# Splitting x2 one token tile at a time, and moving z's load, sums and split to steps 3, 7 and 11 of 16

## The chip, the core and the metric

One NeuronCore of a Trainium2 chip runs the whole program. The metric is device time in microseconds (us), lower is better, given as the median over several runs. TensorE (PE) multiplies, VectorE (DVE), ScalarE (ACT) and GpSimd (POOL) work elementwise, and SyncE (SP) issues nearly all DMA transfers. Each engine takes its instructions strictly in the order in which they are written, and semaphores tie the engines together.

## What is computed

The reference, cut to what matters, with x of 8 x 3072 x 256 values and 24,576 tokens after the transform:

```python
X = np.fft.fft(np.fft.fft(x, axis=1), axis=2).real          # 8 x 3072 x 256
x1 = X.reshape(24576, 256)
h = x1 @ w_in                                                # 256 -> 2048
x2 = (h - np.tanh(h)) @ w_out                                # 2048 -> 256
h2 = x2 @ w_in2                                              # 256 -> 1024
e = np.exp(h2 - h2.max(-1, keepdims=True))
solu = h2 * e / (e.sum(-1, keepdims=True) + 1e-9)
ln = (solu - solu.mean(-1)) / np.sqrt(solu.var(-1) + 1e-6) * g_ln
out = ln @ w_out2                                            # 1024 -> 256
```

## The kernel before

**Stages.** The first stage (24 rounds `q`, some 195 us) computes the Fourier transform over the 3072 positions and leaves its result, z, in DRAM; it also folds the other transform into `w_in` and prepares the weights. The second stage takes the rest of the time: 48 groups `n` of 256 columns of z. One column makes two tokens, so a group is 512 tokens, or four token tiles `i` of 128. Six groups make one batch entry.

**Pieces of twice the precision.** Every matmul is done in three passes on float32r operands, as hi x hi, hi x lo and lo x hi. So every operand has to be split: ACT rounds it (`rnd`, line 151), and POOL or DVE subtracts the rounded part from the whole (`rest`, line 154). Nearly all subtractions in the second stage are POOL's; they all have line 155 in the profile and are told apart by the tile that they write: `gh` (the activations of the first layer pair), `ut` (those of the second), `x2s` (x2) and `zs` (z).

**Steps.** A group has 16 steps `j`, one for each 128 of the 2048 features, and the loop at line 969 writes 768 steps out by hand. In each step PE makes `ab` from the group's `zs` (line 736). DVE makes `h` from it (lines 747 to 763), ACT takes the tanh (line 769), DVE makes `g` (line 774), ACT and POOL split it into `gh`, and two steps later PE adds its product with `w_out` to the group's x2, held in PSUM as `x2p` (function `o1`, line 793). When the sixteenth is in, ACT copies `x2p` to SBUF as `x2f` (line 810), and x2 is split into `x2s`.

**The second layer pair runs one group behind, in cycles of four steps**, one cycle for each token tile. By the remainder q of the step number by 4, PE's order is:

- q = 0: `ab`, `o1`, then the first half of `h2` (line 826, stationary operand `x2s`)
- q = 1: `ab`, the second half of `h2`, `o1`
- q = 2 and 3: `ab`, one half of the last product `po` (line 916, stationary operand `ut`), `o1`

The other engines follow. In q = 0, ACT squares (line 856) and rounds the first `ut`; on POOL the five small instructions of `scale` (lines 863 to 869) need the result of that square, and the first `ut` subtraction stands behind them. `ut` comes from a transposition by way of DRAM (`turn`: one store to `mv_d`, then four loads to `um`). In q = 3, ACT scales the output `o` and SP stores it. A tile's first `h2` is in steps 4, 8, 12 of the next group and 0 of the one behind that.

**z** comes from DRAM to `zf` (function `load_z`, three transfers issued by SP). In three of six groups, those with index 0, 1 and 2 in the batch entry, even and odd parts first have to be added and subtracted on POOL (four instructions of 128 columns, tile `zc`), because the transform leaves them apart; in the other three `zf` is used as it is. Then both 256-column halves u are split into `zs`. All this is for group n + 1 and is done during group n: the load in step 6, the two halves in steps 9 and 11, each with its own sums ahead of it.

**x2** of group n is split at the end of step 1 of group n + 1: two roundings and two subtractions of 128 x 512.

Of the kernel before, what the change touches and what calls it, by code (L numbers as in the profile page):

```python
# [127 lines left out]
def fft2_moe_moe_kernel(  # L128
# [94 lines left out]
    def load_z(n):  # L223
# [13 lines left out]
        zs = zp.tile([P, 2, 2, GP], F32R, tag="zs", name=f"zs{n}")  # L237
        zg[n] = (zf, nb, zs)

    def split_z(n, u):  # L240
        zf, nb, zs = zg[n]
        if n % GPB >= NSJ:
            split_halves(nc.gpsimd, zs[:, 0, u], zs[:, 1, u], zf[:, u])
        else:
            zc = zp.tile([P, GP], F32, tag="zc", bufs=1, name=f"zc{n}_{u}")
            for w, op in enumerate((ALU.add, ALU.subtract)):
                nc.gpsimd.tensor_tensor(out=zc[:, w * P : (w + 1) * P], in0=zf[:, u, :P], in1=zf[:, u, P:], op=op)
            split_halves(nc.gpsimd, zs[:, 0, u], zs[:, 1, u], zc)


    coming, raws = [], {}
# [332 lines left out]
    for q in range(NQ):  # L584
        b, j = divmod(q, NSJ)
        ending = now[:]
        now.clear()
        works = []
        if ahead <= q + 2 < NQ:
            works.append(prep(q + 2))  # L590
        works += ready
        weave(*works)
        weave(*ending)
        ready = coming_weights(q + 1)
        if folds and j == 0:
            fold_w_in(*folds.pop())
        if q == 3:
            transform_nu()
        transform(q)
        if j == NSJ - 1 and q < NQ - 1:  # L600
            evict(b)
        if q == 13:
            for n in range(2):
                load_z(n)
        if q in (15, 16, 17, 18):
            split_z(*divmod((15, 16, 17, 18).index(q), 2))
        if q == NQ - 4:
            nc.sync.dma_start(out=wnu, in_=wnu_d.rearrange("o (m p) -> p (o m)", p=P))
            nc.sync.dma_start(
                out=nu_h, in_=nu_d[:, PAIRS : PAIRS + 1].rearrange("b o -> o b").to_broadcast([P, B])  # L610
            )
# [113 lines left out]
    nc.vector.memset(mhalf, -0.5)  # L725

    hs, ts_, gs = {}, {}, {}
    x2p, x2s = {}, {}

    def ab(n, m):  # L730
        _, nb, zs = zg[n]
# [53 lines left out]
    def o1(n, m):  # L785
        if m == 0:
            x2p[n] = [p_x2.tile([P, 2 * GP], F32, tag=f"x2_{mt}", name=f"x2p{n}_{mt}") for mt in range(2)]
        gh = gs.pop((n, m))
        c, k = divmod(m, 4)

        for i, (hw, hg) in enumerate(((0, 0), (1, 0), (0, 1))):
            for mt in range(2):
                nc.tensor.matmul(  # L793
                    in_pairs(x2p[n][mt]),
                    wo1[c][:, hw, k, mt * P : (mt + 1) * P],
                    in_turn(gh[:, hg]),
                    start=(m == 0 and i == 0),
                    stop=(m == NM - 1 and i == 2),
                )
        if m == NM - 1:  # L800
            xs = wk.tile([P, 2, 2, 2 * GP], F32R, tag="x2s", name=f"x2s{n}")
            x2s[n] = xs
            if n == NG - 1:
                for mt, p in enumerate(x2p.pop(n)):
                    rnd(xs[:, 0, mt], p)
                    rest(nc.vector, xs[:, 1, mt], p, xs[:, 0, mt])
                return
            xf = wk.tile([P, 2, 2 * GP], F32, tag="stage", name=f"x2f{n}")
            for mt, p in enumerate(x2p.pop(n)):
                rnd(xf[:, mt], p)  # L810
            for mt in range(2):
                rnd(xs[:, 0, mt], xf[:, mt])
                rest(nc.gpsimd, xs[:, 1, mt], xf[:, mt], xs[:, 0, mt])

    h2s, es, us, sts, uts, pos, moved = {}, {}, {}, {}, {}, {}, {}

    def h2(n, i, f):
        xs = x2s[n]
        if f == 0:
            h2s[n, i] = taken(bank_h2, [P, FF2], "h2", f"ph2_{n}_{i}")  # L820
        ph = h2s[n, i]
        tk = slice(i * P, (i + 1) * P)
        fs = slice(f * 512, (f + 1) * 512)
        for k in range(2):
            for q, (hx, hw) in enumerate(PASSES):
                nc.tensor.matmul(  # L826
                    in_pairs(ph[:, fs]),
                    xs[:, hx, k, tk],
                    in_turn(wi2[:, hw, k, fs]),
                    start=(k == 0 and q == 0),  # L830
                    stop=(k == 1 and q == 2),
                )
# [98 lines left out]
    def tile_at(step, back):  # L931
        t = (step - NM - back) // 4
        return divmod(t, 4) if 0 <= t < 4 * NG else None
# [35 lines left out]
    for step in range(steps + 2):  # L969
        n, j = divmod(step, NM)  # L970
        if step < steps:
            pab = ab(n, j)
            asb = lead(n, j, pab) if n == 0 else None

        lag = 2 if step < NM else 1
        for s in range(out_done, min(step - lag + 1, steps)):
            act_out(*divmod(s, NM))
        out_done = max(out_done, min(step - lag + 1, steps))
        if step < steps:
            act_in(n, j, pab, asb or lead(n, j, pab))  # L980
# [12 lines left out]
        if step in (10, 12):
            split_wi2((step - 10) // 2)
        if step in (2, 3):
            load_wo2(step - 2)
        if step == 6:
            split_special()
        if 8 <= step < NM:
            gain_wo2(step - 8)  # L1000
        if NM + 2 < step <= NM + 6:
            special_out(step - NM - 3, pa)
        if step == NM:
            cm = mean_wo2()
        if step == NM + 1:
            for half in range(2):
                center_wo2(half, cm)
        if NM + 2 <= step < NM + 6:
            pa = special(step - NM - 2)
        if NM + 2 <= step < NM + 4:  # L1010
            split_wo2(step - NM - 2)
        if j == 6 and 1 <= n and n + 1 < NG:
            load_z(n + 1)
        if 1 <= n and n + 1 < NG and j in (9, 11):
            split_z(n + 1, int(j > 9))


    first.close()
# [81 lines left out]
```

## Time and profile before

| | |
|---|---|
| median of 3 runs | 2838.28 us (2837.79 to 2838.76) |
| the profiled execution | 2839.47 us |
| its span, first to last instruction | 2837.7 us |
| mean granted TensorE clock over the span | 0.996 of full speed |
| PE busy (matmul) | 2742.0 us, 97% |
| DVE / POOL / ACT busy | 84% / 69% / 64% |

The span is what the trace covers; the execution is 1.8 us longer. Idle time of an engine that nobody waits for costs nothing, so the questions are where PE waits, for whom, and why that engine is late.

### The profile page before, as it was taken

The numbers are of one execution on the slowest core, as the hardware profiler recorded it, in microseconds if no ns is written. First come the engines' busy times: TensorE is split into PE (matmuls) and PEld (weight loads), VectorE is DVE, ScalarE is ACT, GpSimd is POOL, SyncE is SP. The second block draws the span as 40 slices with busy tenths as digits, with TensorE's granted clock in tenths as the row PEclk, the third lists the DMA queues.
The fourth block names the chain that finished last, engine by engine and source line by source line (L and its number), as shares of the span: only waits on it lengthen the run. The fifth ranks groups of instructions, "written<-read, shape, count | busy, mean of one in ns | idle before, by whom it ended". The sixth has DMA issues, their size and how long they took to land. (4 is left out here: it accounts for less than half of the span.)

```text
span 2837.7 us, 50135 instructions
## 1 busy us (share of the span) xinstructions
PE 2742.0 (97%) x16799; PEld 2442.4 (86%) x16799; DVE 2394.9 (84%) x4818; ACT 1806.2 (64%) x3287; POOL 1950.6 (69%) x2413
## 2 busy tenths in 40 slices
PE   7899999999999999999999999999999999999998
PEld 4467999889988899889988898889998899888998
DVE  7897888888888888888888888888888888888885
ACT  2336666666666666666666666666666666666665
POOL 0146777777777777777777777777777777777773
PEclk9999999999999999999999999999999999999999
DMA  8780444344434344344434443444434343344441
GB/s 315 241 326 22 97 93 98 91 96 99 96 90 103 90 97 97 90 97 96 99 90 97 97 96 92 101 91 97 97 90 97 90 103 92 95 98 95 94 92 46
DMA packets 876513, 303.77 MB, mean 107 GB/s; under 512 B 788520, under 2 KB 837688, under 8 KB 872960
## 3 DMA queue, kind: packets, MB, share of 16 engines
q1 hardware_dynamic: 873536, 293.95, 41.8%
q10 hardware_dynamic: 2304, 6.29, 0.6%
q8 instruction: 133, 2.18, 0.4%
q14 instruction: 124, 1.02, 0.1%
q0 software_dynamic: 416, 0.33, 0.0%
HBM read 162.01 MB, written 138.47 MB: 106 GB/s over the span
## 5 line engine op out<-in xcount | busy, mean ns | idle before, releaser
L155 POOL TENSOR_TENSOR gh<-g,gh 128x512 fp32r<-128x512 f32 x768 | 984.1, 1285 | 367.4 <-ACT gh L152 357.1
L793 PE MATMUL x2p<-gh,wo 128*128 128x512 f32 x4608 | 1141.6, 381 | 35.8 <-POOL gh L155 22.4
L793 PEld LDWEIGHTS x2p<-gh,wo 128*128 128x128 f32 x4608 | 821.3, 190 | 156.0 <-POOL gh L155 64.5
L769 ACT ACTIVATE t<-h 128x512 f32<-128x512 f32 x768 | 459.1, 598 | 467.6 <-DVE h L763 378.9
L774 DVE TENSOR_TENSOR g<-h,t 128x512 f32<-128x512 f32 x768 | 521.9, 680 | 189.1 <-ACT t L769 183.6
L736 PEld LDWEIGHTS ab<-zs,wt 128*128 128x128 f32 x4608 | 632.9, 191 | 44.2 <-PE ab L736 2.8
L736 PE MATMUL ab<-zs,wt 128*128 128x256 f32 x4608 | 638.8, 275 | 2.3 <-DVE h L763 2.3
L152 ACT ACTIVATE gh<-g 128x512 fp32r<-128x512 f32 x768 | 480.3, 625 | 230.8 <-DVE g L774 228.9
L916 PE MATMUL po<-wo,ut 128*128 128x256 f32 x4608 | 588.5, 276 | 28.1 <-POOL ut L155 24.4
L916 PEld LDWEIGHTS po<-wo,ut 128*128 128x128 f32 x4608 | 549.2, 192 | 37.1 <-POOL ut L155 31.6
L826 PE MATMUL ph<-wi,x2s 128*128 128x512 f32 x2304 | 559.8, 379 | 0.0
L155 POOL TENSOR_TENSOR ut<-um,ut 128x512 fp32r<-128x512 f32 x372 | 478.1, 1285 | 0.9 <-issue 0.9
L747 DVE SCALAR_TENSOR_TENSOR asb<-nb,wnu,ab 128x256 f32<-128x256 f32 x768 | 365.9, 476 | 127.4 <-PE ab L736 120.9
L826 PEld LDWEIGHTS ph<-wi,x2s 128*128 128x128 f32 x2304 | 421.2, 189 | 51.5
L763 DVE TENSOR_TENSOR h<-asb,ab 128x256 f32<-128x256 f32 x768 | 329.5, 429 | 26.5
L762 DVE TENSOR_TENSOR h<-asb,ab 128x256 f32<-128x256 f32 x768 | 329.2, 429 | 26.1
L839 ACT ACTIVATE e<-ph,st 128x1024 f32<-128x1024 f32 x192 | 214.3, 1116 | 88.2 <-PE x2p L793 49.3
L837 DVE TENSOR_REDUCE st<-ph 128x1 f32<-128x1024 f32 x192 | 233.6, 1217 | 3.2 <-PE ph L826 3.2
L845 DVE SCALAR_TENSOR_TENSOR u<-ph,e 128x1024 f32<-128x1024 f32 x192 | 233.5, 1216 | 0.0
L152 ACT ACTIVATE ut<-um 128x512 fp32r<-128x512 f32 x372 | 230.8, 621 | 0.0
L876 DVE STREAM_TRANSPOSE tb<-u 128x1024 f32<-128x1024 f32 x186 | 230.0, 1237 | 0.0
L856 ACT ACTIVATE e<-u,st 128x1024 f32<-128x1024 f32 x192 | 219.7, 1144 | 0.0
(101 smaller groups left out, 1544.0 us busy)
## 6 DMA issues: line engine op xcount, KB each, us to landing
mv_d<-tb SPq DMA_DIRECT2D x186, 512.0 KB, 2.6
um<-mv_d SPq DMA_DIRECT2D x744, 128.0 KB, 3.8
out<-o SPq DMA_DIRECT2D x192, 128.0 KB, 1.7
x<-xr SPq DMA_DIRECT2D x23, 1024.0 KB, 7.8
z_d<-zt ACTq DMA_DIRECT2D x16, 384.0 KB, 6.6
z_d<-zt SPq DMA_DIRECT2D x16, 384.0 KB, 7.5
wo<-w_out SPq DMA_DIRECT2D x24, 256.0 KB, 5.5
zf<-z_d SPq DMA_DIRECT2D x48, 128.0 KB, 3.4
```

What stands on the lines that cost most here:

```text
L152: nc.scalar.activation(out=o, in_=i, func=AF.Copy)
L155: eng.tensor_tensor(out=o, in0=i, in1=hi.bitcast(F32), op=ALU.subtract)
L736: nc.tensor.matmul(in_pairs(pab[:, u]), wt[c][:, hw, u, o : o + P], in_turn(zs[:, hz, u]), start=(i == 0), stop=(i == 2),)
L747: nc.vector.scalar_tensor_tensor(out=asb, in0=zg[n][1], scalar=wnu[:, m : m + 1], in1=pab[:, 0], op0=ALU.mult, op1=ALU.add)
L762: nc.vector.tensor_tensor(out=h[:, 0], in0=asb, in1=pab[:, 1], op=ALU.add)
L763: nc.vector.tensor_tensor(out=h[:, 1], in0=asb, in1=pab[:, 1], op=ALU.subtract)
L769: nc.scalar.activation(out=t, in_=h, func=AF.Tanh)
L774: nc.vector.tensor_tensor(out=g, in0=hs.pop((n, m)).rearrange("p u n -> p (u n)"), in1=ts_.pop((n, m)).rearrange("p u n -> p (u n)"), op=A ...
L793: nc.tensor.matmul(in_pairs(x2p[n][mt]), wo1[c][:, hw, k, mt * P : (mt + 1) * P], in_turn(gh[:, hg]), start=(m == 0 and i == 0), stop=(m = ...
L826: nc.tensor.matmul(in_pairs(ph[:, fs]), xs[:, hx, k, tk], in_turn(wi2[:, hw, k, fs]), start=(k == 0 and q == 0), stop=(k == 1 and q == 2),)
L837: nc.vector.tensor_reduce(out=st[:, 0:1], in_=ph, axis=AX.X, op=ALU.max, negate=True)
L916: nc.tensor.matmul(in_pairs(po[:, :D]), ut[:, hu, ks], in_turn(wo2[:, hw, k]), start=(k == 0 and q == 0), stop=(k == NK2 - 1 and q == 2),)
```

## The change

x2 is no longer split in one go. `x2f` is still copied out in step 1, but every step with q = 3 now ends with the split of the one token tile that `h2` takes in the following step: one rounding and one subtraction of 128 x 256 (two blocks of 128). `x2s` becomes a tile of 128 tokens in four buffers. For the last group, where no steps follow, the split is made straight from PSUM, still in one go but tile by tile (eight roundings and eight subtractions of 128 columns in place of two of 512).

For z, the load moves from step 6 to step 3, all four sums to step 7, and both halves' splits to step 11, behind that step's piece of x2. `zc` gets two buffers. In the first stage the sums of both halves now stand ahead of the first half's split.

```diff
+    zc = {}
+    def sum_z(n):
+        if n % GPB >= NSJ:
+            return
+        zf = zg[n][0]
+        for u in range(2):
+            zc[n, u] = zp.tile([P, GP], F32, tag="zc", name=f"zc{n}_{u}")
+            for w, op in enumerate((ALU.add, ALU.subtract)):
+                nc.gpsimd.tensor_tensor(
+                    out=zc[n, u][:, w * P : (w + 1) * P], in0=zf[:, u, :P], in1=zf[:, u, P:], op=op
+                )
     def split_z(n, u):
         zf, nb, zs = zg[n]
...
-            zc = zp.tile([P, GP], F32, tag="zc", bufs=1, name=f"zc{n}_{u}")
-            for w, op in enumerate((ALU.add, ALU.subtract)):
-                nc.gpsimd.tensor_tensor(out=zc[:, w * P : (w + 1) * P], in0=zf[:, u, :P], in1=zf[:, u, P:], op=op)
-            split_halves(nc.gpsimd, zs[:, 0, u], zs[:, 1, u], zc)
+        split_halves(nc.gpsimd, zs[:, 0, u], zs[:, 1, u], zc.pop((n, u), zf[:, u]))
...
         if q in (15, 16, 17, 18):
-            split_z(*divmod((15, 16, 17, 18).index(q), 2))
+            n, u = divmod((15, 16, 17, 18).index(q), 2)
+            if u == 0:
+                sum_z(n)
+            split_z(n, u)
...
         if m == NM - 1:
-            xs = wk.tile([P, 2, 2, 2 * GP], F32R, tag="x2s", name=f"x2s{n}")
-            x2s[n] = xs
...
-            xf = wk.tile([P, 2, 2 * GP], F32, tag="stage", name=f"x2f{n}")
+            xf = x2f[n] = wk.tile([P, 2, 2 * GP], F32, tag="stage", name=f"x2f{n}")
             for mt, p in enumerate(x2p.pop(n)):
                 rnd(xf[:, mt], p)
-            for mt in range(2):
-                rnd(xs[:, 0, mt], xf[:, mt])
-                rest(nc.gpsimd, xs[:, 1, mt], xf[:, mt], xs[:, 0, mt])
+    def x2s_tile(n, i):
+        x2s[n, i] = wk.tile([P, 2, 2, P], F32R, tag="x2s", bufs=4, name=f"x2s{n}_{i}")
+        return x2s[n, i]
+    def split_x2(n, i):
+        xs, xf = x2s_tile(n, i), x2f[n][:, :, i * P : (i + 1) * P]
+        rnd(xs[:, 0], xf)
+        rest(nc.gpsimd, xs[:, 1], xf, xs[:, 0])
...
-        if j == 6 and 1 <= n and n + 1 < NG:
-            load_z(n + 1)
-        if 1 <= n and n + 1 < NG and j in (9, 11):
-            split_z(n + 1, int(j > 9))
+        if step % 4 == 3:
+            at = tile_at(step + 1, 4)
+            if at:
+                split_x2(*at)
+        if 1 <= n and n + 1 < NG:
+            if j == 3:
+                load_z(n + 1)
+            if j == 7:
+                sum_z(n + 1)
+            if j == 11:
+                for u in range(2):
+                    split_z(n + 1, u)
```

**The order on POOL at a group's start.** These are POOL's instructions in steps 1 to 4 of group 23, before the change (a name's digits: `gh_1` is of step 1, `x2s` is the x2 of the group before; the last number only counts tiles):

```order
L155 TENSOR_TENSOR ut_1_1_17153<-um_1_16940,ut_1_1_17153 128x512
L155 TENSOR_TENSOR x2s_17168<-x2f_17169,x2s_17168 128x512 x2
L155 TENSOR_TENSOR gh_1_17185<-g_1_17183,gh_1_17185 128x512
L155 TENSOR_TENSOR gh_2_17229<-g_2_17227,gh_2_17229 128x512
L155 TENSOR_TENSOR gh_3_17274<-g_3_17272,gh_3_17274 128x512
```

And the same place after it:

```order
L155 TENSOR_TENSOR ut_1_1_17307<-um_1_17091,ut_1_1_17307 128x512
L155 TENSOR_TENSOR gh_1_17334<-g_1_17332,gh_1_17334 128x512
L155 TENSOR_TENSOR gh_2_17378<-g_2_17376,gh_2_17378 128x512
L155 TENSOR_TENSOR x2s_0_17414<-x2f_17322,x2s_0_17414 128x256
L155 TENSOR_TENSOR gh_3_17432<-g_3_17430,gh_3_17432 128x512
```

The two long x2 subtractions no longer stand ahead of `gh_1`; one piece of half their width stands between `gh_2` and `gh_3`, and its like ahead of `gh_7`, `gh_11` and `gh_15`.

**The order on POOL where z is prepared.** Group 23 prepares a group that needs the sums. Before, from step 8 to step 12:

```order
L155 TENSOR_TENSOR ut_3_0_17474<-um_3_17293,ut_3_0_17474 128x512
L155 TENSOR_TENSOR gh_8_17499<-g_8_17497,gh_8_17499 128x512
L155 TENSOR_TENSOR ut_3_1_17509<-um_3_17293,ut_3_1_17509 128x512
L247 TENSOR_TENSOR zc_0_17524<-zf_17390 128x128 x2
L155 TENSOR_TENSOR zs_17395<-zc_0_17524,zs_17395 128x256
L155 TENSOR_TENSOR gh_9_17538<-g_9_17536,gh_9_17538 128x512
L155 TENSOR_TENSOR gh_10_17580<-g_10_17578,gh_10_17580 128x512
L247 TENSOR_TENSOR zc_1_17616<-zf_17390 128x128 x2
L155 TENSOR_TENSOR zs_17395<-zc_1_17616,zs_17395 128x256
L155 TENSOR_TENSOR gh_11_17630<-g_11_17628,gh_11_17630 128x512
```

After, from step 7 to step 12 (lines 880 to 886 are `scale`, lines 863 to 869 before):

```order
L155 TENSOR_TENSOR x2s_1_17593<-x2f_17322,x2s_1_17593 128x256
L249 TENSOR_TENSOR zc_0_17596<-zf_17417 128x128 x2
L249 TENSOR_TENSOR zc_1_17599<-zf_17417 128x128 x2
L155 TENSOR_TENSOR gh_7_17611<-g_7_17609,gh_7_17611 128x512
...
L155 TENSOR_TENSOR gh_10_17736<-g_10_17734,gh_10_17736 128x512
L155 TENSOR_TENSOR x2s_2_17772<-x2f_17322,x2s_2_17772 128x256
L155 TENSOR_TENSOR zs_17422<-zc_0_17596,zs_17422 128x256
L155 TENSOR_TENSOR zs_17422<-zc_1_17599,zs_17422 128x256
L155 TENSOR_TENSOR gh_11_17788<-g_11_17786,gh_11_17788 128x512
```

The sums left the place behind `ut_3_1` and stand one step after `gh_6`, behind a piece of x2.

**The order on ACT at the same place.** Before, steps 9 to 11 of group 23:

```order
L152 ACTIVATE ut_3_1_17509<-um_3_17293 128x512
L152 ACTIVATE zs_17395<-zc_0_17524 128x256
L152 ACTIVATE gh_9_17538<-g_9_17536 128x512
L769 ACTIVATE t_10_17546<-h_10_17543 128x512
L839 ACTIVATE e_1_17563,st_1_17561<-ph_22_1_17483,st_1_17561 128x1024
```

After, step 9, and then the end of step 11:

```order
L152 ACTIVATE ut_3_1_17670<-um_3_17451 128x512
L152 ACTIVATE gh_9_17694<-g_9_17692 128x512
L779 ACTIVATE t_10_17702<-h_10_17699 128x512
...
L942 ACTIVATE o_3_17758<-po_3_17704,st_3_17357 128x256
L152 ACTIVATE x2s_2_17772<-x2f_17322 128x256
L152 ACTIVATE zs_17422<-zc_0_17596 128x256
L152 ACTIVATE zs_17422<-zc_1_17599 128x256
L152 ACTIVATE gh_11_17788<-g_11_17786 128x512
```

The rounding of `zs`, which needs POOL's sums, no longer stands ahead of the tanh of step 10; both roundings stand behind `o`, four steps after their sums.

## Rows read from the trace of the kernel before

**Rows 1.** The page's busy time, share of the span, instructions.

```profile
PE 2742.0 (97%) x16799; PEld 2442.4 (86%) x16799; DVE 2394.9 (84%) x4818; ACT 1806.2 (64%) x3287; POOL 1950.6 (69%) x2413
```

**Rows 2.** Busy time by cycle: group 25's first, third, fourth; group 26's third.

```profile
core 0: us, PE busy (x) PEld busy (x) DVE busy (x) ACT busy (x) POOL busy (x), PEclk, DMA share, GB/s
1541.07:1554.96 13.89, 13.39 (x85) 12.09 (x84) 12.14 (x29) 10.25 (x20) 10.63 (x13) 1.00 0.37 85
...
1568.09:1581.69 13.60, 13.43 (x86) 12.11 (x85) 9.99 (x22) 7.65 (x15) 9.13 (x14) 1.00 0.56 120
1581.69:1596.11 14.42, 13.37 (x86) 12.19 (x85) 12.79 (x25) 9.85 (x18) 11.66 (x15) 1.00 0.35 82
...
1623.13:1636.26 13.13, 13.13 (x86) 12.17 (x85) 11.45 (x24) 8.79 (x18) 9.55 (x12) 1.00 0.41 93
```

**Rows 3.** The same view of group 28: its first and last cycle.

```profile
1702.66:1716.75 14.09, 13.44 (x85) 12.13 (x84) 12.68 (x33) 10.26 (x20) 10.63 (x14) 1.00 0.36 84
...
1743.25:1756.62 13.37, 13.37 (x85) 12.24 (x84) 11.98 (x28) 8.82 (x17) 9.58 (x12) 1.00 0.38 88
```

**Rows 4.** Timeline, group 25, steps 1 to 3: start, length, instruction, idle before.

```profile
1550.62 2.52 POOL L155 TENSOR_TENSOR x2s<-x2f,x2s 128x512 fp32r<-128x512 f32 x2
...
1554.43 0.70 PE L793 MATMUL x2p<-gh,wo 128*128 128x512 f32 x2 [0.50 <-POOL gh L155]
```

**Rows 5.** Timeline, group 24, steps 10 and 14.

```profile
1523.47 0.50 ACT L152 ACTIVATE zs<-zc 128x256 fp32r<-128x256 f32 x1 [3.76 <-POOL zc L247]
...
1535.25 1.38 PE L916 MATMUL po<-wo,ut 128*128 128x256 f32 x10 [1.05 <-POOL ut L155]
```

**Rows 6.** Timeline, group 25, steps 7 to 10, by engine.

```profile
1567.66 0.47 ACT L925 ACTIVATE o<-po,st 128x256 f32<-128x256 f32 x1
1569.29 0.63 ACT L152 ACTIVATE gh<-g 128x512 fp32r<-128x512 f32 x1 [1.17 <-DVE g L774]
...
1570.00 1.28 POOL L155 TENSOR_TENSOR gh<-g,gh 128x512 fp32r<-128x512 f32 x1 [1.91 <-ACT gh L152]
1572.53 0.19 POOL L864 TENSOR_TENSOR st<-st 128x1 f32<-128x1 f32 x1 [1.10 <-ACT e L856]
1573.90 1.28 POOL L155 TENSOR_TENSOR ut<-um,ut 128x512 fp32r<-128x512 f32 x1
...
1570.06 1.46 PE L826 MATMUL ph<-wi,x2s 128*128 128x512 f32 x6
1575.28 1.50 PE L916 MATMUL po<-wo,ut 128*128 128x256 f32 x12
```

**Rows 7.** Tiles x2s, zf and zc: duration in ns (min/median/max), first and last start.

```profile
L152 ACT ACTIVATE x2s<-x2f x94: 626/639/650, 242.5 to 2743.0; 128x512 fp32r<-128x512 f32 x94
L155 POOL TENSOR_TENSOR x2s<-x2f,x2s x94: 1268/1290/1327, 243.2 to 2745.8; 128x512 fp32r<-128x512 f32 x94
...
L247 POOL TENSOR_TENSOR zc<-zf x96: 447/464/902, 148.8 to 2561.2; 128x128 f32<-128x128 f32 x96
L152 ACT ACTIVATE zs<-zc x48: 439/504/578, 150.2 to 2561.7; 128x256 fp32r<-128x256 f32 x48
L155 POOL TENSOR_TENSOR zs<-zc,zs x48: 739/744/11208, 150.7 to 2562.4; 128x256 fp32r<-128x256 f32 x48
```

**Rows 8.** Timeline, SP's queue in group 25, steps 3 to 6.

```profile
1554.19 0.34 SPq L927 DMA_DIRECT2D out<-o  x1
1558.41 0.33 SPq L878 DMA_DIRECT2D mv_d<-tb  x1
...
1566.44 1.19 SPq L232 DMA_DIRECT2D zf<-z_d  x2
```

**Rows 9.** Timeline, group 1, steps 3 and 4.

```profile
250.82 2.42 POOL L155 TENSOR_TENSOR wo<-wg,wo 128x1024 fp32r<-128x1024 f32 x1
251.89 1.46 PE L826 MATMUL ph<-wi,x2s 128*128 128x512 f32 x6
```

**Rows 10.** Timeline, behind the last step.

```profile
2794.06 1.29 DVE L155 TENSOR_TENSOR x2s<-x2p,x2s 128x512 fp32r<-128x512 f32 x2 [4.63 <-ACT x2s L152]
```

More of the change, by code (lines that the diff above doesn't have):

```diff
@@ L238, in load_z @@
         zg[n] = (zf, nb, zs)
+    zc = {}
[9 more added lines that the diff above has]
+                )
     def split_z(n, u):
         zf, nb, zs = zg[n]
-        if n % GPB >= NSJ:
-            split_halves(nc.gpsimd, zs[:, 0, u], zs[:, 1, u], zf[:, u])
-        else:
-            zc = zp.tile([P, GP], F32, tag="zc", bufs=1, name=f"zc{n}_{u}")
-            for w, op in enumerate((ALU.add, ALU.subtract)):
-                nc.gpsimd.tensor_tensor(out=zc[:, w * P : (w + 1) * P], in0=zf[:, u, :P], in1=zf[:, u, P:], op=op)
-            split_halves(nc.gpsimd, zs[:, 0, u], zs[:, 1, u], zc)
+        split_halves(nc.gpsimd, zs[:, 0, u], zs[:, 1, u], zc.pop((n, u), zf[:, u]))
     coming, raws = [], {}
@@ L727, in fft2_moe_moe_kernel @@
     hs, ts_, gs = {}, {}, {}
-    x2p, x2s = {}, {}
+    x2p, x2f, x2s = {}, {}, {}
     def ab(n, m):
@@ L800, in o1 @@
         if m == NM - 1:
-            xs = wk.tile([P, 2, 2, 2 * GP], F32R, tag="x2s", name=f"x2s{n}")
-            x2s[n] = xs
             if n == NG - 1:
-                for mt, p in enumerate(x2p.pop(n)):
-                    rnd(xs[:, 0, mt], p)
-                    rest(nc.vector, xs[:, 1, mt], p, xs[:, 0, mt])
+                ps2 = x2p.pop(n)
+                for i in range(4):
+                    xs = x2s_tile(n, i)
+                    for mt, p in enumerate(ps2):
+                        tk = slice(i * P, (i + 1) * P)
+                        rnd(xs[:, 0, mt], p[:, tk])
+                        rest(nc.vector, xs[:, 1, mt], p[:, tk], xs[:, 0, mt])
                 return
-            xf = wk.tile([P, 2, 2 * GP], F32, tag="stage", name=f"x2f{n}")
+            xf = x2f[n] = wk.tile([P, 2, 2 * GP], F32, tag="stage", name=f"x2f{n}")
             for mt, p in enumerate(x2p.pop(n)):
                 rnd(xf[:, mt], p)
-            for mt in range(2):
-                rnd(xs[:, 0, mt], xf[:, mt])
-                rest(nc.gpsimd, xs[:, 1, mt], xf[:, mt], xs[:, 0, mt])
+    def x2s_tile(n, i):
[5 more added lines that the diff above has]
+        rest(nc.gpsimd, xs[:, 1], xf, xs[:, 0])
     h2s, es, us, sts, uts, pos, moved = {}, {}, {}, {}, {}, {}, {}
     def h2(n, i, f):
-        xs = x2s[n]
+        xs = x2s[n, i]
         if f == 0:
@@ L821, in h2 @@
         ph = h2s[n, i]
-        tk = slice(i * P, (i + 1) * P)
         fs = slice(f * 512, (f + 1) * 512)
@@ L827, in h2 @@
                     in_pairs(ph[:, fs]),
-                    xs[:, hx, k, tk],
+                    xs[:, hx, k],
                     in_turn(wi2[:, hw, k, fs]),
```

## The prediction, made before the changed kernel had run

> **What bounds the kernel now.** I began with the busy times of the whole span: PE has a matmul in flight in 97% of it and no other engine comes near [rows 1]. A busy matmul is not a matmul at its peak, so this says where to look, not how much there is. For that I cut the steady part into cycles of four steps, from the first `ab` matmul of one cycle to that of the next, and read each one's length beside PE's busy time [rows 2]. In the third cycle of group 26 both are 13.13 us: there PE streams without a hole. Second cycles are 13.13 us long as well, and so are third and fourth cycles in groups that prepare z without sums; group 26's third holds both splits of such a z, so those cost nothing where they stand. Four such cycles make a group of 52.52 us: PE's floor, which nothing in this change lowers, since it takes no matmul away.
>
> What stands above the floor is what the change can win. First cycles take 13.89 us, 0.76 above. In groups that prepare a z with sums (group 25 is one) the third and fourth cycles take 13.60 and 14.42 us, together 1.76 above. In groups with index 4 in the batch entry DVE has one more copy in each step, and their last cycle takes 13.37 us with no z sums in it [rows 3]: a floor of their own, which the change leaves.
>
> The timeline gives each excess its cause. In the first cycle POOL spends 2.52 us on x2's two subtractions, ahead of the `gh` pieces of steps 2 and 3, and PE's `x2p` matmuls then wait on `gh` [rows 4]. In the third, ACT stands 3.76 us before the rounding of `zs`, because the sums are behind two long pieces on POOL; the tanh of the next step is queued behind that rounding, so the whole chain of the first layer slips. The second half does the same to POOL itself, and in step 14 PE waits 1.05 us for the low part of `ut` [rows 5].
>
> **The change, part by part.** *Where the new work falls.* A cycle has one loose place, between q = 3 and the next q = 0. ACT ends `o` at 1568.13 and sits idle for 1.17 us until it begins `gh` at 1569.29; POOL sits idle for 1.91 us until 1570.00 [rows 6]. The new piece of x2 comes right behind `o`. The trace has no x2 piece 256 wide; the nearest are the `zs` pieces, 0.50 us on ACT and 0.74 on POOL, and the upper bounds are the pieces 512 wide, 0.64 and 1.29 [rows 7]. I take the `zs` rows, which have the same width. So: rounding from 1568.1 to 1568.6, about 0.1 to the next engine, subtraction from 1568.7 to 1569.4. `h2` begins at 1570.06 and needs the low part in its third matmul, about 0.43 later (six take 1.3), at 1570.5. The margin is 1.1 us, and with the upper bounds still 0.4. POOL is done 0.6 before `gh` comes. Cost: 0.
>
> [...]
>
> *z's sums* are four instructions of 0.46 us [rows 7], about 1.74 together, now behind the x2 piece of step 7: 1569.4 to 1571.2. `gh` then starts 1.2 later than it did, at 1571.2, and ends at 1572.4; the first instruction of `scale` takes some 0.2, as the second does, and the second, which had to wait 1.10 us for ACT's square until 1572.53, can begin near 1572.6. So the chain to `ut` is late by 0 to 0.1. `ut` ended at 1575.18, and `po`, begun at 1575.28, needs its low part in its third matmul, 0.25 later: 0.3 of margin. Cost: 0. With x2 at its upper bounds POOL is 0.7 later, 0.4 of it beyond the margin: 21 groups make 9 us. `gh` itself goes to the `o1` behind both halves of `h2`, which is after 1570.06 and twice 1.3, 1572.7.
>
> *Both z splits in step 11* give ACT the x2 piece and two of 0.50, to 1569.6 at the latest: `gh` is 0.3 late; the tanh behind it waits for DVE's `h`, which doesn't depend on it. POOL has 0.74 three times from 1568.7: `gh` begins at 1570.9, 0.9 late, less than the 1.10 us idle before `scale`. Cost: 0. Nothing is left that waits for the sums: they are four steps old.
>
> *z's load in step 3.* SP issues it behind `o`'s store at 1554.19. The two `zf` transfers took 1.19 us to issue in step 6, a third follows; the next store, of `mv_d`, stood at 1558.41 [rows 8]. There are 3.9 us for some 2: nothing behind it is held up, and the sums come four steps later. Cost: 0.
>
> *What is won.* First cycles: 30 groups between 2 and 46 by 0.76 are 22.8. Seven with index 5 start with a cycle as long as group 28's first, 14.09 us, since DVE's delay spills into them; I let it come down to group 28's last, 13.37: 5.0, and 0.7 for group 47. The eight with index 4 now have 14.09, 13.13 and twice 13.37, or 53.96 us, and go to four of 13.37: 3.8. z: 21 groups by 1.76 are 37.0. Together 69.3 us.
>
> *What is lost.* In group 1 the split of `w_out2` fills POOL until 1.35 us after the first `h2` began [rows 9]. The x2 piece, done long before so far, now stands behind it, and ends at 253.98 where `h2`'s third matmul wants it at 252.3: 1.7 us once, bounds 0 and 2.5. Behind the last step DVE's two subtractions take 1.29 us [rows 10]; eight small ones, with eight roundings before them, end later, by 0 (the elements are the same) to 4 us (each as long as one of 512 in that row, less the two), and the softmax of the tile before waits behind them. I take 1, nearer the lower end. In the first stage the sums of one z move ahead of another's split, beside PE that has other work: 0.
>
> The sum is 69.3 - 1.7 - 1.0 = 66.6 us off the profiled 2839.47: 2772.9. That execution is 1.2 above the median shown, so I predict 2772 us.
>
> **The rivals.** *A: POOL's debt comes back one cycle earlier.* Step 7 packs the x2 piece and all sums into one idle stretch. If they take longer than worked out, `ut` is late in step 10 as it now is in step 14, at up to 1.29 us (14.42 less 13.13) in 21 groups, 27 us at most: up to 2799; what ends above 2782 I count as A. Against it: the margin of 0.3 and the constant durations in rows 7 (464 in the median; the 902 ns are in the first stage). For it: the margin is thin.
>
> *B: one half doesn't come.* ACT's two copies to `x2f` stay in step 1. If these, not POOL's subtractions, delay the first cycle, the 32 us of first cycles stay: 2804. Against: in rows 4 POOL is busy with x2 just before the `gh` that PE waits for. Were the z half missing, 2809.
>
> *C: no change.* PE's 13.13 us might be regained idle time after a delay, with DVE the true limit. Then the lengths stay: 2838. Against: DVE is busy 11.45 of 13.13 us in the cleanest cycle, and undisturbed cycles follow each other at 13.13.
>
> *D: slower.* The x2 piece could be locked out on POOL by DVE's run of instructions in that stretch. If it ended 1.1 us later, PE would begin to wait in every `h2`, 188 times; 67 us by 188 is 0.36, so from 1.5 us late on the kernel is slower. Held for 2.0 us it costs 188 by 0.9 = 169 us: 2941. The trace speaks against it: the 94 long subtractions of x2 ran beside DVE all the time, from 1268 to 1327 ns. Only in the first stage did a `zs` piece take 11.2 us [rows 7]. [...]
>
> **How the numbers follow.** The forecast, without returning waits, 74%, with a range of its own from 2764 (the losses 0, and two thirds of the 7.7 us that index 4 would keep above the floor gone too) to 2782 (the 9 us of the x2 piece's upper bounds, and 1 more of the losses). A 13%, B 6%, C 3%, D 4%. Up to 2790 the range holds the forecast and half of A, 80%. Within 0.2% of the time before (5.7 us, about what a measurement of this kernel tells from nothing) lies C, 3%; slower is D, 4%; the rest, 93%, is faster.
>
> **What would show it.** First, third and fourth cycles of 13.1 us in the changed kernel, and 13.4 in index 4; ACT's 3.76 us before `zs` gone; the x2 pieces near 0.50 and 0.74 us, done before `h2` begins; no wait of PE on `ut` in steps 10 and 14, and little on `gh`. The forecast is wrong if `h2` waits on POOL's `x2s` (B or D by its size), if PE waits on `ut` in step 10 (A), or if the cycles stay above 13.13 with DVE's chain as the releaser (C).

## The result, and the profile after

| | before | after |
|---|---|---|
| median | 2838.44 us (2837.79 to 2838.76, 4 runs) | 2770.2 us (2766.54 to 2772.77, 4 runs) |
| the profiled execution | 2839.47 us | 2769.12 us |
| its span | 2837.7 us | 2767.3 us |
| mean granted TensorE clock | 0.996 | 0.995 |

The ratio is 0.9759, 95% interval 0.9742 to 0.9776: some 68 us less, where 66 had been forecast. (With one more run the kernel before stands at 2838.44 in place of 2838.28.) Lines 793, 826, 837, 863 and 916 of the kernel before are now 803, 843, 854, 880 and 933.

PE's matmul time falls by 20 us although it does the same 16,799 matmuls: a run of matmuls that a wait breaks in two counts for more busy time than the same run in one piece. Twelve `po` matmuls in one run take 1.50 us [rows 6]; in [rows 5] the two ahead of the wait take 0.39 and the ten behind it 1.38. The line answers to [rows 1]:

```profile
PE 2722.0 (98%) x16799; PEld 2449.5 (89%) x16799; DVE 2389.8 (86%) x4824; ACT 1824.2 (66%) x3387; POOL 1968.7 (71%) x2507
```

The same cycles as in [rows 2] and [rows 3]: group 25's four, group 26's third, group 28's first and last (columns as there).

```profile
1504.11:1517.24 13.13, 13.13 (x85) 12.16 (x84) 11.45 (x24) 9.59 (x20) 9.57 (x12) 1.00 0.40 92
1517.24:1530.37 13.13, 13.13 (x85) 12.16 (x84) 11.45 (x24) 8.73 (x18) 9.58 (x12) 1.00 0.52 120
1530.37:1543.50 13.13, 13.13 (x85) 12.16 (x84) 11.45 (x24) 8.73 (x18) 11.20 (x17) 1.00 0.39 92
1543.50:1556.63 13.13, 13.13 (x85) 12.16 (x84) 11.45 (x24) 9.53 (x20) 10.94 (x14) 1.00 0.39 91
1582.89:1596.02 13.13, 13.13 (x85) 12.16 (x84) 11.45 (x24) 8.72 (x18) 9.55 (x12) 1.00 0.40 92
1661.67:1674.83 13.16, 13.16 (x85) 12.20 (x84) 11.87 (x28) 9.39 (x19) 9.41 (x12) 1.00 0.39 92
1701.77:1715.13 13.36, 13.36 (x86) 12.24 (x85) 11.97 (x28) 9.54 (x19) 10.94 (x14) 1.00 0.39 90
```

The 13.89, 13.60 and 14.42 us are all 13.13 now, PE streaming from end to end, although POOL has 11.20 us of work in the third cycle, 2.07 more than before. Its work grew there and PE did not notice: the place counts, not the load. Only groups of index 4 stay clearly above the floor; in groups 2 to 46 everything else is 13.13 to 13.16 us on average.

The loose place between step 6 and step 7 of group 25, which answers to [rows 6], in the timeline:

```profile
1529.93 0.47 ACT L942 ACTIVATE o<-po,st 128x256 f32<-128x256 f32 x1
1530.29 0.42 ACT L152 ACTIVATE x2s<-x2f 128x256 fp32r<-128x256 f32 x1
1530.78 0.73 POOL L155 TENSOR_TENSOR x2s<-x2f,x2s 128x256 fp32r<-128x256 f32 x1 [0.41 <-ACT x2s L152]
1531.47 1.71 POOL L249 TENSOR_TENSOR zc<-zf 128x128 f32<-128x128 f32 x4
1532.12 1.27 PEld L843 LDWEIGHTS ph<-wi,x2s 128*128 128x128 f32 x6
1532.34 1.46 PE L843 MATMUL ph<-wi,x2s 128*128 128x512 f32 x6
1533.13 1.29 POOL L155 TENSOR_TENSOR gh<-g,gh 128x512 fp32r<-128x512 f32 x1
1534.81 0.19 POOL L881 TENSOR_TENSOR st<-st 128x1 f32<-128x1 f32 x1 [0.24 <-ACT e L873]
1536.18 1.29 POOL L155 TENSOR_TENSOR ut<-um,ut 128x512 fp32r<-128x512 f32 x1
1537.56 1.50 PE L933 MATMUL po<-wo,ut 128*128 128x256 f32 x12
```

The order is as forecast, and the pieces are done somewhat sooner: the x2 piece stands right behind `o` and is done 0.83 us before `h2` starts; the four sums behind it take 1.71 us; `gh` comes 0.85 us later against `h2` than in [rows 6] (forecast 1.2); and the second instruction of `scale` still waits for ACT's square, 0.24 us where it was 1.10, so the chain to `ut` is not late.

The tile x2s, which answers to [rows 7] and [rows 10] (duration in ns, min/median/max; first and last start):

```profile
L152 ACT ACTIVATE x2s<-x2f x188: 404/417/425, 249.1 to 2715.2; 128x256 fp32r<-128x256 f32 x188
L155 POOL TENSOR_TENSOR x2s<-x2f,x2s x188: 726/733/741, 252.8 to 2715.7; 128x256 fp32r<-128x256 f32 x188
L152 ACT ACTIVATE x2s<-x2p x8: 272/277/282, 2720.4 to 2722.6; 128x128 fp32r<-128x128 f32 x8
L155 DVE TENSOR_TENSOR x2s<-x2p,x2s x8: 281/292/293, 2720.7 to 2722.9; 128x128 fp32r<-128x128 f32 x8
```

The 188 pieces cost what the `zs` rows had said or less, 417 and 733 ns, without one slow one among them.

SP at step 3 of group 25, behind the store of `o`, which answers to [rows 8]:

```profile
1517.68 0.98 SPq L232 DMA_DIRECT2D zf<-z_d  x2
1518.70 0.47 SPq L236 DMA_DIRECT2D nb<-nu_d  x1
1520.88 0.33 SPq L895 DMA_DIRECT2D mv_d<-tb  x1
```

The load is issued by 1519.17, 1.7 us before the next store is due.

**The account.** Cycles are measured as in the prediction, from the first `ab` matmul of one to that of the next, and summed over the groups named; the stretches around them go by the first `asb` of a group.

| stretch | forecast, us | measured, us |
|---|---|---|
| first cycles, index 0 to 3, 30 groups | -22.8 | -23.0 |
| first cycles, index 5, 7 groups | -5.0 | -6.5 |
| index 4, 8 groups | -3.8 | -6.0 |
| third and fourth cycles with sums, 21 groups | -37.0 | -37.8 |
| group 47 | -0.7 | -0.9 |
| group 1 | +1.7 | +1.6 |
| behind the last step | +1.0 | +2.7 |
| first stage and group 0 | 0 | -0.5 |
| sum | -66.6 | -70.4 |

The spans differ by 70.3 us. The first stage moves by several us from one execution to the next (the first `asb` comes at 195.5 to 201.2 us in the profiles of this study), so 0.5 there means nothing.

### The profile page after: what moved, and what is told of

It is laid out like the page before. It is cut to its first block, busy times and chain, and to the rows that moved or that the text cites. A ratio compares the mean times of both kernels' runs of the same rounds, so it can differ in the third digit from the quotient of the medians.

```text
span 2767.3 us, 50637 instructions
## 1 busy us (share of the span) xinstructions
PE 2722.0 (98%) x16799; PEld 2449.5 (89%) x16799; DVE 2389.8 (86%) x4824; ACT 1824.2 (66%) x3387; POOL 1968.7 (71%) x2507
## 3 DMA queue, kind: packets, MB, share of 16 engines
q14 instruction: 127, 1.04, 0.1%
## 5 line engine op out<-in xcount | busy, mean ns | idle before, releaser
L803 PE MATMUL x2p<-gh,wo 128*128 128x512 f32 x4608 | 1124.5, 380 | 6.1 <-POOL gh L155 2.9
```

The costliest lines, as they stand in the source:

```text
L803: nc.tensor.matmul(in_pairs(x2p[n][mt]), wo1[c][:, hw, k, mt * P : (mt + 1) * P], in_turn(gh[:, hg]), start=(m == 0 and i == 0), stop=(m = ...
```

## The experiments

**1. Each half alone.** `e1_x2_alone` has the new split of x2 and prepares z as before; `e2_z_alone` the reverse (with one buffer for `o` in place of two).

```diff
 # e1_x2_alone, against the changed kernel
...
-        if 1 <= n and n + 1 < NG:
-            if j == 3:
-                load_z(n + 1)
-            if j == 7:
-                sum_z(n + 1)
-            if j == 11:
-                for u in range(2):
-                    split_z(n + 1, u)
+        if j == 6 and 1 <= n and n + 1 < NG:
+            load_z(n + 1)
+        if 1 <= n and n + 1 < NG and j in (9, 11):
+            split_z(n + 1, int(j > 9))
 # e2_z_alone, against the changed kernel
...
+            for mt in range(2):
+                rnd(xs[:, 0, mt], xf[:, mt])
+                rest(nc.gpsimd, xs[:, 1, mt], xf[:, mt], xs[:, 0, mt])
...
-        if step % 4 == 3:
-            at = tile_at(step + 1, 4)
-            if at:
-                split_x2(*at)
```

> x2 is split tile by tile as in the changed kernel, z stays as it was before (load in step 6, each half's sums and split in steps 9 and 11). Theory of two independent gains: first cycles fall from 13.89 to 13.13 us in all groups, 46 by some 0.76 or 35 us; the two z excesses of 1.76 us in 21 groups stay; with the losses of group 1 and of the end, 3 to 4 us, about 2807 us. Rival, the two halves need each other: the x2 pieces of steps 7 and 11 now stand on POOL ahead of the sums of steps 9 and 11, so the fourth cycle's wait on ut grows by the piece's 0.73 us in 21 groups: 2822 us.

> z moved as in the changed kernel, x2 split in one go in step 1 as before (the tile o has one buffer, since the two tiles of sums need the room). Theory of two independent gains: third and fourth cycles of the groups with sums fall to 13.13 us, 21 by 1.76 or 37 us, and first cycles stay at 13.89: about 2802 us. Rival, the sums only come out free because x2's pieces also evened out POOL: some of the 1.76 stays, and the time lies between 2802 and 2838.

x2 alone: 2813.42 us, ratio 0.991 (0.9893 to 0.9926), between the theory and its rival. z alone: 2803.19 us, ratio 0.9874 (0.9859 to 0.9888). The kernel before took 2839.24 on this chip, so the parts bring 25.8 and 36.0 us. Each half clears its own cycles: with x2 alone the first cycles are 13.13 to 13.17 us on average, with z alone the third and fourth are at the floor and the first stay at 13.90 to 13.93 (index 4 and 5, at 14.08 and 14.09, apart). Together they bring 69.5 on this chip (the next run), 7.6 more than the parts. The profile of x2 alone shows where: fourth cycles with sums rise from 14.47 us on average to 14.82, 0.34 by 21 groups, or 7.2 us. This is its timeline of POOL, PE and PE's weight loads (PEld) in the fourth cycle of group 24, which begins at 1512.58:

```profile
1514.48 0.73 POOL L155 TENSOR_TENSOR x2s<-x2f,x2s 128x256 fp32r<-128x256 f32 x1 [0.57 <-ACT x2s L152]
1514.54 1.85 PE L833 MATMUL ph<-wi,x2s 128*128 128x512 f32 x6
1515.17 0.87 POOL L247 TENSOR_TENSOR zc<-zf 128x128 f32<-128x128 f32 x2
1515.26 0.73 PEld L833 LDWEIGHTS ph<-wi,x2s 128*128 128x128 f32 x4 [0.51 <-POOL x2s L155]
1516.66 0.75 POOL L155 TENSOR_TENSOR zs<-zc,zs 128x256 fp32r<-128x256 f32 x1 [0.62 <-ACT zs L152]
...
1521.59 1.38 PE L923 MATMUL po<-wo,ut 128*128 128x256 f32 x10 [1.04 <-POOL ut L155]
```

The new piece starts 0.06 us before `h2`, where the changed kernel's starts 1.56 us before it: on ACT it stands behind a tanh and an `o` that are late from the third cycle, in which ACT still stands idle for 3.76 us before the rounding of `zs`. So `h2` waits for the piece, and its six matmuls take 1.85 us in place of 1.46. The piece also stands ahead of the second half's sums on POOL, and the first `ut` ends 8.95 us after the cycle's start, where it was 8.57 in the kernel before. PE then waits for `ut` as long as in [rows 5], 1.04 us for 1.05, because it comes there 0.39 us later itself. By these times either delay alone would have made the cycle some 0.4 us longer. Moving the sums away is thus worth more after the x2 change than before it.

**2. The early sums alone.** In `e3_halves_back` the sums stay in step 7, and the halves are split in steps 9 and 11 as before.

```diff
-            if j == 11:
-                for u in range(2):
-                    split_z(n + 1, u)
+            if j in (9, 11):
+                split_z(n + 1, int(j > 9))
```

> The changed kernel with the two halves of z split in steps 9 and 11 again; only the sums stay in step 7 and the load in step 3. Theory: what cost time was ACT's rounding standing behind sums that POOL had not begun, so early sums alone win the whole 37 us: 2770 us, as the changed kernel. Rival, the place counts: a half split in step 9 puts its 0.74 us on POOL in the middle of its two ut pieces, and half of the excess comes back: near 2788 us.

2769.77 us, ratio 0.9755 (0.9741 to 0.977): the time of the changed kernel, cycles outside index 4 at 13.13 to 13.16 us on average. All of z's gain comes from the sums standing ahead of time; between these two places of the splits there is no difference. The load stands earlier here too, but is no cause of its own: in the trace of the kernel before, no `zc` instruction on POOL waited for its load.

**3. Place or size.** `e8_pieces_step1` cuts x2 into the same four pieces, but leaves all of them in step 1 (with a fifth buffer for `x2s`).

```diff
             for mt, p in enumerate(x2p.pop(n)):
                 rnd(xf[:, mt], p)
+            for i in range(4):
+                split_x2(n, i)
...
-        x2s[n, i] = wk.tile([P, 2, 2, P], F32R, tag="x2s", bufs=4, name=f"x2s{n}_{i}")
+        x2s[n, i] = wk.tile([P, 2, 2, P], F32R, tag="x2s", bufs=5, name=f"x2s{n}_{i}")
...
-        if step % 4 == 3:
-            at = tile_at(step + 1, 4)
-            if at:
-                split_x2(*at)
```

> The changed kernel's z and its four x2 pieces of 256 columns, but all four issued in step 1 where x2 was split before. Theory: the place wins, not the size; POOL spends 4 by 0.73 = 2.9 us there, 0.4 more than on the two long ones, so first cycles grow to 14.3 us: 46 by 1.17 over the changed kernel, 2770 + 54 = 2824 us. Rival: short pieces let gh through in time, and the time stays near 2770, at most near the 2803 of z alone.

2817.01 us, ratio 0.9916 (0.9903 to 0.993). The timeline of its ACT, POOL and PE in the first cycle of group 24:

```profile
1482.46 0.61 ACT L152 ACTIVATE gh<-g 128x512 fp32r<-128x512 f32 x1
1483.05 2.81 POOL L155 TENSOR_TENSOR x2s<-x2f,x2s 128x256 fp32r<-128x256 f32 x4
...
1485.82 2.51 POOL L155 TENSOR_TENSOR gh<-g,gh 128x512 fp32r<-128x512 f32 x2
1487.14 0.70 PE L803 MATMUL x2p<-gh,wo 128*128 128x512 f32 x2 [0.76 <-POOL gh L155]
```

First cycles are 14.15 us in most groups: the same wait as in [rows 4], 0.26 longer than before (0.76 for 0.50), for 0.29 us more of POOL work (2.81 in place of 2.52). ACT's roundings of x2 stay in step 1 as well, but they are not what PE waits for: ACT had rounded this `gh` by 1483.07, and POOL, busy with x2 until then, took it up at 1485.82. Cutting wins nothing by itself and costs its fixed parts; the place wins.

**4. How much room the new places have.** `e4_x2_twice` and `e5_x2_thrice` make each x2 subtraction on POOL two and three times over, with the same result.

```diff
-        rest(nc.gpsimd, xs[:, 1], xf, xs[:, 0])
+        for _ in range(2):    # 3 in e5_x2_thrice
+            rest(nc.gpsimd, xs[:, 1], xf, xs[:, 0])
```

> The changed kernel with every x2 subtraction on POOL done twice (0.73 us more in each of 188 cycles, same values). Theory of the margins read in the changed kernel's trace: 1.26 us between the piece's end and h2's third matmul, so h2 never waits; behind the sums 0.24 us are left before scale and 0.34 before po, together 0.58, so there ut is 0.15 us late in 21 groups: 0 to 4 us, 2770 to 2774. Rival D's cliff is nearer: if h2 or gh waits in every cycle, each 0.1 us costs 19, and 0.73 without margin 137 us: 2907.

> The changed kernel with every x2 subtraction on POOL done three times (1.46 us more in each cycle, same values). After the doubled one: the trace there showed 0.22 us of margin behind the sums and 0.48 behind the z splits, before PE waits on ut. The theory that rival D named a real edge, only farther off than one piece: h2 now waits too, 0.3 to 0.5 us in 188 cycles, 56 to 94 us, and ut in cycles with sums or z splits by 18 and 26 us more: 2870 to 2910 us, slower than before the change. Rival: waits in one cycle cover those of the next and the cost grows as from the first doubling, 24 us more: near 2820.

Twice: 2794.11 us, ratio 0.984 (0.9825 to 0.9855), 24 us longer than `e3_halves_back` on the same chip. At most 4 us had been expected, so the room was over-read. `h2` does not wait, but third cycles with sums are 13.64 us (+0.51), and fourth cycles in which z is split 13.38 (+0.25). The timeline of POOL, PE's weight loads and matmuls for the former, in group 24, the doubled piece of step 7 and then step 10:

```profile
1493.92 1.54 POOL L155 TENSOR_TENSOR x2s<-x2f,x2s 128x256 fp32r<-128x256 f32 x2 [0.42 <-ACT x2s L152]
...
1499.98 1.29 POOL L155 TENSOR_TENSOR ut<-um,ut 128x512 fp32r<-128x512 f32 x1
...
1500.59 0.30 PEld L934 LDWEIGHTS po<-wo,ut 128*128 128x128 f32 x2
1500.69 0.39 PE L934 MATMUL po<-wo,ut 128*128 128x256 f32 x2
...
1501.32 1.19 PEld L934 LDWEIGHTS po<-wo,ut 128*128 128x128 f32 x10 [0.43 <-POOL ut L155]
1501.32 1.38 PE L934 MATMUL po<-wo,ut 128*128 128x256 f32 x10 [0.24 <-POOL ut L155]
```

`ut` is stationary here: the load of the third matmul's weights stands idle for it from 1500.89 on, 0.43 us, and the matmul from 1501.08 on, 0.24 us. The second piece begins only 0.81 us after the first (two take 1.54 us, one takes 0.73), so POOL was pushed by 0.81 us; the cycles grew by 0.51 and 0.25. So the changed kernel has 0.30 us of room behind the sums and 0.56 behind z's splits. 21 third cycles and 45 fourth ones make 22 us, where groups 2 to 46 took 21.4 more than in the changed kernel; 6 more us of the profiled execution are in group 1, where the clock fell (below).

Thrice: 2917.13 us, ratio 1.0269 (1.025 to 1.0288), slower than before and 7 us above the range expected. Here is `h2` in its timeline, group 24, step 0:

```profile
1527.26 2.35 POOL L155 TENSOR_TENSOR x2s<-x2f,x2s 128x256 fp32r<-128x256 f32 x3 [0.93 <-ACT x2s L152]
...
1528.82 0.59 PE L844 MATMUL ph<-wi,x2s 128*128 128x512 f32 x2
...
1529.67 0.73 PEld L844 LDWEIGHTS ph<-wi,x2s 128*128 128x128 f32 x4 [0.66 <-POOL x2s L155]
```

The first two matmuls run, the third's weights wait: the picture that rival D drew. Undisturbed cycles are 13.65 us, 0.52 longer; two more pieces push POOL by 1.62 us (2.35 less 0.73), so `h2` has 1.10 us of room. Third cycles with sums take 14.42 and fourth ones 14.18, 1.29 and 1.05 longer; the rooms of 0.30 and 0.56 would give 1.32 and 1.06. `e1_x2_alone` agrees: there the piece of step 11 was 1.5 us late, and `h2` lost 0.39.

**5. The ends.** `e6_ends` makes the last group's split in two pieces of 512 again, and puts the first x2 piece of group 0 into step 17, ahead of `w_out2`'s split. `e7_ends_copy` also moves the column copy of index 4 from DVE to ACT.

```diff
-                ps2 = x2p.pop(n)
+                xl = [wk.tile([P, 2, 2 * GP], F32R, tag="stage", name=f"x2l{n}_{w}") for w in range(2)]
+                for mt, p in enumerate(x2p.pop(n)):
+                    rnd(xl[0][:, mt], p)
+                    rest(nc.vector, xl[1][:, mt], p, xl[0][:, mt])
                 for i in range(4):
-                    xs = x2s_tile(n, i)
-                    for mt, p in enumerate(ps2):
-                        tk = slice(i * P, (i + 1) * P)
-                        rnd(xs[:, 0, mt], p[:, tk])
-                        rest(nc.vector, xs[:, 1, mt], p[:, tk], xs[:, 0, mt])
+                    x2s[n, i] = [a[:, :, i * P : (i + 1) * P] for a in xl]
...
+        if step == NM + 1:
+            split_x2(0, 0)
         if step % 4 == 3:
             at = tile_at(step + 1, 4)
-            if at:
+            if at and step != NM + 3:
...
 # e7_ends_copy alone
-            nc.vector.tensor_copy(
-                out=h[:, 1, SPECIAL_C : SPECIAL_C + 1], in_=a1536[:, m, b : b + 1]
-            )
+            rnd(h[:, 1, SPECIAL_C : SPECIAL_C + 1], a1536[:, m, b : b + 1])
```

> The changed kernel with its two losses taken out: the last group's x2 is split in two roundings and two subtractions of 512 as before, and the very first x2 piece stands in step 1 of group 1, ahead of the split of w_out2. Theory: the end gets 2.1 us back (first h2 behind the last step at 16.1 in place of 18.3 us after its last asb) and group 1 1.7: about 2766 us. Rival: the clock's drops decide both places (the granted clock was 0.66 in group 1 and 0.55 to 0.60 at the end of the changed kernel's profiled run), and the time stays at 2770 within its scatter.

> As the one with both losses taken out, and in groups of index 4 the one-column copy into h is ACT's instead of DVE's. Theory: DVE's 16 copies of 0.16 us hold these groups at 53.16 us; ACT has room, so they fall to 52.52: 8 by 0.64, 5 us less than that kernel, about 2761. Rival: the copy in ACT stands between h and the tanh and puts 0.2 us on the chain of the first layer, and nothing is won.

> The changed kernel once more, on the same chip as the next run, to compare the two directly: their runs so far were on different chips, whose times for the kernel before differ by 2 to 3 us. Expected 0.9755 to 0.976 of the kernel before, 2770 us on a chip where that takes 2839. If the lower clock behind the last step and in group 1 is the changed kernel's own, its profile shows it again in the same two places; if it comes and goes, the executions differ by the 2 to 4 us that it costs.

> The kernel with the split behind the last step in two pieces again and the column copy of index 4 on ACT, beside the changed kernel. If both edits hold: shorter by 2.7 us (the end back from 54.50 to 51.8 us) and by 3.8 us (8 groups of index 4, from 53.3 to 52.8), about 6 us or 0.2%; interval below that of the changed kernel. If what the first comparison showed was the difference of the chips, the two come out the same.

`e6_ends`: 2768.13 us, ratio 0.9748 (0.9734 to 0.9761), which the intervals don't tell from the changed kernel. `e7_ends_copy`: 2764.46 us, ratio 0.9729 (0.9716 to 0.9742). To compare the two on one chip they ran again: `e9_after_beside`, the changed kernel, 2770.21 us (2767.79 to 2772.4), ratio 0.9749 (0.9736 to 0.9762); `e10_best_beside`, the same as `e7_ends_copy`, 2762.69 us (2762.05 to 2763.74), ratio 0.9725 (0.9712 to 0.9738). No run of the one reaches one of the other: the second is shorter by 7.5 us, or 0.27%, and is the fastest version of this study. The end accounts for 2.7 us of it (54.50 us from the last `asb` to the end in both profiles of the changed kernel, 51.81 and 51.80 in `e7_ends_copy` and `e10_best_beside`, 51.82 before). Index 4 gives 3.8: with the copy on ACT these eight groups take 52.80 us on average, and 53.28 without. The rest is within what the first stage moves. Group 1 gained nothing from the earlier piece (below).

**The two ends in the trace of the changed kernel.** Its timeline behind the last step: ACT's first pieces, DVE's reduction for the softmax of the tile before, which stands behind DVE's pieces, and `po`:

```profile
2720.43 1.77 ACT L152 ACTIVATE x2s<-x2p 128x128 fp32r<-128x128 f32 x6 [1.17 <-PE x2p L803]
2723.11 1.22 DVE L854 TENSOR_REDUCE st<-ph 128x1 f32<-128x1024 f32 x1
2727.19 4.17 PE L933 MATMUL po<-wo,ut 128*128 128x256 f32 x22 [0.24 <-DVE ut L155]
```

In the kernel before the same three stood so:

```profile
2793.43 1.09 ACT L152 ACTIVATE x2s<-x2p 128x512 fp32r<-128x512 f32 x2 [1.16 <-PE x2p L793]
2795.27 1.22 DVE L837 TENSOR_REDUCE st<-ph 128x1 f32<-128x1024 f32 x1
2799.41 2.72 PE L916 MATMUL po<-wo,ut 128*128 128x256 f32 x22 [0.24 <-DVE ut L155]
```

And PE's busy time and the granted clock there in the changed kernel, in the view by stretches (columns as in [rows 2]):

```profile
2722.83:2727.00 4.17, 2.62 (x22) 2.19 (x20) 2.05 (x4) 2.55 (x6) 0.00 (x0) 1.00 0.04 15
...
2728.00:2730.00 2.00, 2.00 (x13) 2.00 (x12) 1.25 (x5) 0.00 (x0) 0.19 (x1) 0.55 0.00 0
```

The reduction starts 2.68 us after the first rounding, and in the kernel before 1.84: the eight small pieces cost 0.84 us. Then comes what the prediction has no term for. PE was busy for only 2.62 of 4.17 us (3.23 at the same place in the kernel before), then the granted clock fell to 0.55, and 22 `po` matmuls took 4.17 us where they took 2.72 before: 1.45 us. The two make 2.3 of the 2.7 us.

Group 1 has two ways to the same loss. The timeline of the changed kernel, `o1` and the first `h2`, which answers to [rows 9]:

```profile
250.14 2.77 PE L803 MATMUL x2p<-gh,wo 128*128 128x512 f32 x6
252.71 1.99 PE L843 MATMUL ph<-wi,x2s 128*128 128x512 f32 x6
...
252.79 0.73 POOL L155 TENSOR_TENSOR x2s<-x2f,x2s 128x256 fp32r<-128x256 f32 x1
```

Its busy times and clock in this stretch:

```profile
250.00:255.00 5.00, 5.00 (x20) 3.80 (x20) 2.55 (x8) 1.24 (x3) 5.00 (x5) 0.66 0.00 0
```

And the timeline of `e1_x2_alone` at the same place:

```profile
249.46 1.46 PE L793 MATMUL x2p<-gh,wo 128*128 128x512 f32 x6
250.76 0.59 PE L833 MATMUL ph<-wi,x2s 128*128 128x512 f32 x2
252.91 1.13 PE L833 MATMUL ph<-wi,x2s 128*128 128x512 f32 x4 [1.56 <-POOL x2s L155]
```

With the clock at 1.00, as in `e1_x2_alone`, `h2` waits 1.56 us for the late piece, which is the forecast. In the changed kernel the clock was at 0.66 there, `o1` took 2.77 us in place of 1.46, and by the time of `h2`'s third matmul the piece was there. In `e6_ends` the piece was early and the clock still fell (0.71), and the group, from its first `asb` to the next group's, took 60.5 us; it took 60.6 in the changed kernel and 59.0 in the kernel before. `e2_z_alone`, which splits x2 as before, took 60.5 too: the fall alone costs what group 1 lost.

## Why the prediction was right, point by point

**The bound and the floor** held. PE's floor is 13.13 us, and every cycle that was above it for want of `gh` or `ut` came down to it; C, idle time regained, is out.

**First cycles and z with sums** were sized to within 1 us each (23.0 for 22.8, 37.8 for 37.0), because both were lengths read from cycles of the same trace, not added up from instructions. That x2's place on POOL is the cause is shown by `e8_pieces_step1`; that for z it is the early sums, by `e3_halves_back`. Both halves of rival B's condition were put to the test by experiment 1: the times with one half missing, forecast as 2804 and 2809, are 2803.2 and 2813.4; the second misses that without early sums the x2 piece of step 11 is late itself.

**Index 4 and 5** were sized too low, 12.5 us measured for 8.8. I let first cycles of index 5 come down to group 28's last, 13.37, since DVE's delay spills into them; they came to 13.16. And index 4 was not held at 13.37 in all four cycles: its first is 13.16. `e7_ends_copy` shows that DVE's copy makes most of what is left there, 0.48 of 0.76 us in a group; the rest was not traced further.

**Step 7** was the thin place, as stated: 0.3 us of margin, less up to 0.1. Experiment 4 measures 0.30. So A did not come, but by 0.30 us; the x2 piece at its upper bounds, some 0.8 us later in all, would have cost time. My expectation for `e4_x2_twice`, made after seeing the changed kernel's trace, was worse than the prediction: it took 0.58 for this room, read at the matmul and not at the load of its weights, counted the second piece as 0.73 us where it pushed POOL by 0.81, and had no term for the fourth cycles, 45 by 0.25 or 11 us.

**`h2`** was given 1.1 us of room, and it has 1.10. That a late piece makes `h2` wait, as D had it, is shown by `e5_x2_thrice` (0.52 us in each undisturbed cycle), but no piece of the changed kernel was held up: all 188 on POOL took 726 to 741 ns. That DVE locks POOL out was a guess of mine, which no run shows as the cause; what the trace of the kernel before has is one `zs` piece in the first stage that took 11.21 us, with DVE busy for 11.18 of them. D's edge, slower from a piece 1.5 us late, is too far out, as D counted only `h2`: `ut` waits long before `h2` does. By the rooms measured, a delay d above 1.10 us lengthens the 180 cycles of groups 2 to 46 by d - 1.10, but 21 third cycles by d - 0.30 and 45 fourth ones by d - 0.56. At 1.62 that makes 135 us, where these groups took 134 more than in the changed kernel; by the same sum the 70 us won are gone at an estimated 1.26 us.

**What the pieces cost.** The traces show a part that does not shrink with a piece's width: behind the last step eight pieces of 128 on DVE took 292 ns each, where a quarter of a long one in [rows 10], 1.29 us for two, is 161. POOL's pieces show such a part too, 2.81 us for four in step 1 in place of 2.52 for two. In the loose place it costs nothing (cycles of 13.13 us), behind the last step the small pieces cost 0.84 us, near the 1.0 taken, and in step 1 (`e8_pieces_step1`) POOL's part is the 0.26 us lost in each group.

**Group 1 and the end** came out at 4.3 us for 2.7. The terms were right where the clock stayed up (1.56 for 1.7 in `e1_x2_alone`, and 0.84 for 1.0). That PE's clock can fall here, and make 22 `po` matmuls 1.45 us longer, was missing. Group 1's 1.6 for 1.7 is luck: in the changed kernel `h2` did not wait there, and the fall of the clock cost as much. In the sum too errors of both signs met: index 4 and 5 gave 3.7 us more than forecast, and the end took 1.7 more.

## What to carry to other kernels

Look for the loose place in a cycle, on each engine of the chain, and put work there that is ready early; in another place the same work made PE wait in every group (0.76 us a first cycle), and cutting it up without moving it only added its fixed parts (0.26 us more). Before filling such a place, read the room at every consumer behind it, and at the load of the weights where the late tile is stationary: one place had 1.10, 0.56 and 0.30 us of room, depending on who came next. When such a room is measured by doing an instruction twice, take the push from start to start (0.81 us here), not the length of one (0.73). And a place is loose only while the chain ahead of it is in time: without the early sums a moved piece came 1.5 us late, and the parts alone brought 62 us, together 69.5.

## What the runs showed of the hardware

In groups 2 to 46 the granted clock was 1.00 in the kernel before and in the changed kernel, in each of six stretches that cover them. It fell at two places shortly after PE had waited. Behind the last step it was 0.66 on average from 14 to 19 us after the last `asb` in six of the seven profiles with the eight small pieces, and 1.00 in all five with the two long ones. The exception is `e4_x2_twice`, where it was 1.00 from 10 to 24 us after the last `asb`. In two with the long pieces it fell later, to 0.90 from 33 to 43 us after it in `e2_z_alone` and to 0.93 from 37 to 43 us in `e6_ends`; their ends took 53.3 and 53.4 us, where the other three took 51.8. What PE did ahead of it does not separate these: in the 4 us before, PE was busy for 2.16 in `e4_x2_twice`, without a fall behind it, and for 2.96 in `e5_x2_thrice`, with one.

In group 1 the clock fell in every profile, to between 0.50 and 0.71 over its lowest 5 us, but for those of the kernel before and of `e1_x2_alone` (1.00), the two that prepare z as before. Most kernels have one profile here, so that the fall belongs to z's new order is not shown. PE's work does not separate these either: in the 5 us before, PE was busy for 4.09 in the kernel before, without a fall, and for 4.09 in `e2_z_alone`, with one; for 3.83 in `e1_x2_alone`, without, and for 3.82 in the changed kernel, with one. What decides it stays open.
